# Moving the ranks' matmul to the state's PSUM bank, the row comparisons to GpSimd, and one transposition ahead of four

## The chip, the cores and the metric

The kernel runs on one core of one Trainium2 chip. The metric is the device time of one execution in microseconds. Four compute engines take part: TensorE (PE in the profile; PEld is its weight load), VectorE (DVE), ScalarE (ACT) and GpSimd (POOL). SyncE (SP) issues most of the DMAs.

## The reference

Three layers follow each other. The second routes each of 2304 token rows to one of eight experts; the third mixes all eight experts for each row.

```python
# q, k, v: (4, 8, 576, 64); x has 2304 rows of 512 columns; 8 experts, hidden width 1024
gamma = 1.0 - 2.0 ** (-5.0 - np.arange(H))
Dmat = np.where(rel >= 0, gamma[:, None, None] ** rel[None], 0.0)
x = (scale * (q @ k.T) * Dmat) @ v                   # retention, per batch and head
...
logits = x @ w_gate; e = argmax(logits)               # first mixture: the best expert
out[row] = softmax(logits)[e] * (relu(x[row] @ w1[e]) @ w2[e])
...
P = exp(logits2 - max); 8 rounds: P /= P.sum(1) + 1e-9; P /= P.sum(0) + 1e-9; P *= N / E
out += P[:, e:e+1] * (relu(x @ w1[e]) @ w2[e])        # second mixture: all experts
```

## The kernel before

The rows are worked in 18 tiles of 128 rows. The first sixteen (t = 0 to 15) are four chunks of each of the four batches, and carry a running state `st[b]` per batch; the last two hold the remaining 64 rows of two batches each. One loop over t runs the retention of tile t and, one tile behind it, the routing of tile t - 1. The order of the instructions on each engine is the order in which the program writes them: nothing is rearranged, and an engine that waits holds up all that stands behind it in its own queue.

One turn of the loop issues, in this order:

- `scale(t + 2)`: GpSimd multiplies k by its decays (L376) and q by its own (L379, `qs`), each over 128x512.
- `scores(t + 1)`: TensorE multiplies k and q (L391), VectorE applies the decay mask (L397, `sc`).
- `logits(t - 1)`: TensorE multiplies the tile's output by the gate's weights (L470) into columns 0 to 127 of PSUM bank 7; ScalarE copies them to `L` (L473).
- `states(t)`: TensorE applies the state to `qs` (L409), from the fifth tile on.
- `xtrans(t - 1)`: TensorE transposes the tile's output in four steps (L446) into bank 1.
- `route_a(t - 1)`: TensorE transposes `L` (L478) into columns 128 to 255 of bank 7. VectorE reduces it (L480), takes the maximum and its index (L483, L484, L486), makes the one-hot row `ohb` (L488) and the difference `sh` (L490).
- `new_state(t)`: TensorE multiplies k and v (L421) into bank 5; VectorE adds them to the state (L427, or a copy, L429, in the first chunk).
- `enlist(t - 2)`: TensorE collects the token numbers of an earlier tile from `at` and `row` (L532).
- `route_e(t - 1)`, `attend(t)`: ScalarE's exponential (L496), VectorE's gate (L497, L499); TensorE multiplies scores and v (L437), and ScalarE copies the result out (L440).
- `route_b(t - 1)`: two matmuls (L504, L505) count the rows per expert ahead of each row, into columns 256 to 271 of bank 7. VectorE turns the counts into a place (L510 to L513), splits it into `high` and `low` (L515 to L517) and makes two `row` tables of 24 columns (L523). GpSimd makes `at` over 128 columns (L521).
- `xout(t - 1)`: ScalarE scales the tile's output (L452), SP writes it to DRAM (L455).

From the twelfth tile on the same turns also split the first expert's weights into a high and a low part: ScalarE casts (L256), VectorE and GpSimd subtract half each (L233). After the loop, the first mixture's matmuls begin while the last tile's routing ends; then a table of the experts' order is made, and the rest of the weights are loaded.

A PSUM bank has one buffer. A new tile in a bank may be written only when all accesses to the tile before it are over. The lines touched here:

```python
p = d["pr"][:, 256:256 + 2 * E].rearrange("p (a e) -> p a e", a=2)   # route_b: bank 7, with the logits
nc.tensor.matmul(p[:, 0, :], ltb, d["ohb"], start=True, stop=True)
```

Of the kernel before, what the change touches and what calls it, by code (L numbers as in the profile page):

```python
# [13 lines left out]
ALU = mybir.AluOpType  # L14
# [21 lines left out]
def kernel(  # L36
# [18 lines left out]
    nc = tc.nc  # L55
    N, DM = out.shape
    E, _, F = w11.shape
    NT = N // 128
# [34 lines left out]
    def bank(i, shape=(128, 512)):  # L93
        return psum.tile(list(shape), F32, tag=f"b{i}", name=f"b{i}")
# [27 lines left out]
    tokf = const.tile([128, 2, NT], F32, name="tokf")  # L122
    places = const.tile([128, NT], F32, name="places")
    iota = const.tile([128, 128], F32, name="iota")
    tile0 = const.tile([128, E, 3], F32, name="tile0")
# [38 lines left out]
    def part(src, make):  # L164
        raws.append([src, make, None, 0])
        return len(raws) - 1
# [32 lines left out]
    for p in range(1):  # L199
        for e in range(E):  # L200
            for j in range(2):
                pr = [part((e, j, h), lambda e, j, h: w21[e][:, h * half + 256 * j:h * half + 256 * (j + 1)]
                           .rearrange("(k p) f -> p k f", p=128)) for h in range(2)]
# [104 lines left out]
    with ExitStack() as at:  # L308
# [7 lines left out]
        T = {}  # L316
# [53 lines left out]
        def scale(t):  # L370

            d = T[t]
            ch = t // B
            if ch < NCH:
                f = cs[:, C_KS + ch * H:C_KS + (ch + 1) * H].unsqueeze(2).to_broadcast([128, H, D])
                nc.gpsimd.tensor_tensor(d["k"], d["k"], f, ALU.mult)  # L376
            if ch:
                d["qs"] = wk.tile([128, 4, 128], F32, tag="qs", name="qs")
                nc.gpsimd.tensor_tensor(d["qs"], d["qT"], qdec[ch], ALU.mult)  # L379
# [20 lines left out]
        def states(t):  # L400

            d = T[t]
            ch = t // B
            d["xT"] = xp = bank(4 if t % 2 else 0, (128, 4, 128))
            if ch:
                for r in range(4):
                    off = 0
                    for b, s, n in tiles[t]:
                        nc.tensor.matmul(xp[:, r, off:off + n], st[b][:, r, :], d["qs"][:, r, off:off + n],  # L409
                                         start=r == 0 and off == 0, stop=False, skip_group_check=True)  # L410
                        off += n

        def new_state(t):

            d = T[t]
            ch = t // B
            if ch < NCH:
                sp = bank(5, (128, 4, 64))
                for h in range(H):
                    g = slice(64 * (h % 2), 64 * (h % 2) + 64)  # L420
                    nc.tensor.matmul(sp[g, h // 2, :], d["k"][:, h, :], d["v"][:, h, :], start=True, stop=True,  # L421
                                     tile_position=(0, 64 * (h % 2)))
                s = st[tiles[t][0][0]]
                for lo in (0, 64):
                    o = s[lo:lo + 64, :, lo:lo + 64]
                    if ch:
                        nc.vector.tensor_tensor(o, sp[lo:lo + 64], o, ALU.add)  # L427
                    else:
                        nc.vector.tensor_copy(o, sp[lo:lo + 64])  # L429
# [12 lines left out]
        def xtrans(t):  # L442
            d = T[t]
            d["xp"] = p = bank(1 if t < NT - 1 else 4, (128, 4, 128))
            for r in range(4):
                nc.tensor.transpose(p[:, r, :], d["xT"][:, r, :], ident)  # L446
# [18 lines left out]
        def logits(t):  # L465
            d = T[t]
            d["pr"] = bank(7)
            p = d["pr"][:, 0:128]
            for r in range(KB):
                nc.tensor.matmul(p[32 * r:32 * r + 32, :], wg1[:, r, :], d["xT"][:, r, :], start=True, stop=True,  # L470
                                 tile_position=(0, 32 * r))
            d["L"] = wk.tile([128, 128], F32, tag="L", name="L")
            nc.scalar.copy(d["L"], p)  # L473

        def route_a(t):
            d = T[t]
            p = d["pr"][:, 128:256]
            nc.tensor.transpose(p, d["L"], ident)  # L478
            lg = wk.tile([128, E], F32, tag="lgs", name="lgs")
            nc.vector.tensor_reduce(lg, p.rearrange("p (k e) -> p e k", k=4)[:, 0:E, :], AX.X, ALU.add)  # L480
            m8 = wk.tile([128, 8], F32, tag="m8", name="m8")
            i8 = wk.tile([128, 8], U32, tag="i8", name="i8")
            nc.vector.max(m8, lg)  # L483
            nc.vector.max_index(i8, m8, lg)  # L484
            fi = wk.tile([128, 1], F32, tag="fi", name="fi")
            nc.vector.tensor_copy(fi, i8[:, 0:1])  # L486
            ohb = d["ohb"] = wk.tile([128, E], BF16, tag="ohb", name="ohb")
            nc.vector.tensor_scalar(ohb, cs[:, C_EXP:C_EXP + E], fi, None, ALU.is_equal)  # L488
            sh = d["sh"] = wk.tile([128, E], F32, tag="sh", name="sh")
            nc.vector.tensor_scalar(sh, lg, m8[:, 0:1], None, ALU.subtract)  # L490
# [9 lines left out]

        def route_b(t):
            d = T[t]
            p = d["pr"][:, 256:256 + 2 * E].rearrange("p (a e) -> p a e", a=2)
            nc.tensor.matmul(p[:, 0, :], ltb, d["ohb"], start=True, stop=True)  # L504
            nc.tensor.matmul(p[:, 1, :], onesb, d["ohb"], start=True, stop=True)  # L505
            t1 = wk.tile([128, E], F32, tag="t1", name="t1")
            pf = places[:, t:t + 1]
            low = wk.tile([128, 1], F32, tag="low", name="low")
            high = wk.tile([128, 1], F32, tag="high", name="high")
            nc.vector.tensor_tensor(t1, p[:, 0, :], base, ALU.add)  # L510
            nc.vector.tensor_tensor(t1, t1, d["ohb"], ALU.mult)
            nc.vector.tensor_reduce(pf, t1, AX.X, ALU.add)
            nc.vector.tensor_tensor(base, p[:, 1, :], base, ALU.add)  # L513

            nc.vector.tensor_scalar(high, pf, -63.5, 1.5 * 2.0 ** 30, ALU.add, ALU.add)  # L515
            nc.vector.tensor_scalar(high, high, -1.5 * 2.0 ** 30, None, ALU.add)
            nc.vector.tensor_tensor(low, pf, high, ALU.subtract)  # L517

            d["at"] = wk.tile([128, 128], BF16, tag="at", name="at")
            d["row"] = wk.tile([128, 2, E, 3], BF16, tag="row", name="row")  # L520
            nc.gpsimd.tensor_scalar(d["at"], iota, low, None, ALU.is_equal)  # L521
            for i in range(2):
                nc.vector.tensor_scalar(d["row"][:, i], tile0, high, tokf[:, i, t:t + 1], ALU.is_equal, ALU.mult)  # L523

        listed = []

# [402 lines left out]
        for t in range(NT):  # L929
            if t + 2 < NT:  # L930
                scale(t + 2)
            if t == NT - 1:
                states(t)
            if t:
                scores(t + 1)
                logits(t - 1)
            if t < NT - 1:
                states(t)
            if t:
                xtrans(t - 1)  # L940
                route_a(t - 1)
            table_step()
            presplit(t, 0)
            new_state(t)
            table_step()
            presplit(t, 1)
            if t == NT - 1:
                gtrans(0, 0)
            if t > 1:
                enlist(t - 2)  # L950
                if t == GAT1:
                    first_ids(1)
            if t:
                route_e(t - 1)
            attend(t)
            if t + 2 < NT and len(tiles[t + 2]) > 1:

                nc.gpsimd.memset(sc[t % 2][0:64, :, :, 64:128], 0.0)
            if t:
                route_b(t - 1)  # L960
                if t == GAT1:
                    gather(0, 1, 2)
                if t < NT - 1:
                    xout(t - 1)
            if n_known[0]:
                n_known[0] = min(8, n_known[0] + KN[max(0, t - PICK_AT - 1)])
                load_more()
            if t == PICK_AT:
                table.append(early_table())
            if t == IDX0:  # L970
                first_ids(0)
            if t == GAT1 - 1:
                early_tokens()
            table_step()
            presplit(t, 2)
            load(t + 4)
            table_step()
            presplit(t, 3)
            if t == GAT0:
                gather(0, 0, 1)  # L980
# [332 lines left out]
    for g in range(n_unit):  # L1313
        pe, i = divmod(g, 4)
        p, e = divmod(pe, E)
# [163 lines left out]
    for s in range(E, n_exp):  # L1479
        p, e = divmod(s, E)  # L1480
# [254 lines left out]
    while ready:  # L1735
        t = ready.pop()
# [66 lines left out]
    while n_done < len(tasks):  # L1803
        moved = True
        while moved:
            moved = False
            while ends and ends[0][0] <= t_now + 1e-9:
                _, _, t = heapq.heappop(ends)
# [12 lines left out]
            for k in at:  # L1821
                if at[k] > t_now + 1e-9:
                    continue
                if k == "PE":
                    if n_pe[0] < len(line) and not waits[line[n_pe[0]]]:
                        t = line[n_pe[0]]
# [105 lines left out]
```

## Time and profile before

| what | value |
| --- | --- |
| time, median of 3 runs | 1841.89 us (1840.78 to 1845.59) |
| time of the profiled execution | 1840.57 us |
| its span, first to last instruction | 1838.7 us |
| PE busy, share of the span | 1803.2 us, 98% |
| DVE busy | 1235.5 us, 67% |
| ACT busy | 892.0 us, 49% |
| POOL busy | 567.3 us, 31% |
| mean granted TensorE clock | 0.998 |

The busy shares are averages over stages with different limits: the loop over the 18 tiles is the first 119 us or so, and what follows is the two mixtures. Times in the rows below are microseconds from the start of the span. The 1.87 us between the span and the execution's time lie around it.

### The profile page before, as it was taken

Reading aid. Unit: us, or ns where it says so; the run is one execution under the profiler, and the core shown is the slowest. Engines: PE = TensorE matmul, PEld = TensorE weight load, DVE = VectorE, ACT = ScalarE, POOL = GpSimd, SP = SyncE. Lnnn points to the kernel's source line nnn. Section 1 sums busy time; section 2 is a strip of 40 time slices with the busy share of each in tenths; the row PEclk is TensorE's granted clock in tenths of the full one; section 3 lists DMA queues with packets and bytes.
Section 4 is the critical chain, followed back from the end, with each engine's and each line's share of the span. In section 5 each row is a group of like instructions: output and inputs, shape, how many; then the busy total and the mean of one; then the engine's idle time right before and its main releaser. Section 6 shows DMA issues by size and latency. Waiting matters only on the chain.

```text
span 1838.7 us, 32928 instructions
## 1 busy us (share of the span) xinstructions
PE 1803.2 (98%) x12265; PEld 1721.5 (94%) x12265; DVE 1235.5 (67%) x2313; ACT 892.0 (49%) x1718; POOL 567.3 (31%) x582
## 2 busy tenths in 40 slices
PE   8889999999999999999999999999999999999998
PEld 7769999999899999999899999999999999999997
DVE  7984456547645554554467777778877777777778
ACT  2344456544434343434455555555655555555554
POOL 4455577532432323334311112111323111111212
PEclk9999999999999999999999999999999999999999
DMA  8755556564454556444755555655455545555540
GB/s 293 252 174 193 184 185 205 193 204 177 152 215 161 205 173 224 177 178 163 258 158 163 164 158 174 192 155 155 144 173 190 159 155 161 169 155 165 155 127 35
DMA packets 190455, 325.05 MB, mean 177 GB/s; under 512 B 20534, under 2 KB 93383, under 8 KB 190284
## 3 DMA queue, kind: packets, MB, share of 16 engines
q1 hardware_dynamic: 186716, 312.20, 52.0%
q0 software_dynamic: 3136, 9.95, 1.6%
q8 instruction: 99, 1.62, 0.4%
q10 hardware_dynamic: 432, 0.69, 0.1%
q14 instruction: 72, 0.59, 0.1%
HBM read 248.26 MB, written 74.53 MB: 176 GB/s over the span
## 4 chain that ended last, share of the span: by engine, by line
PE 85%; DVE 3%; issue 2%; ACT 1%; POOL 0%; DMA 0%; POOLq 0%; ACTq 0%; DVEq 0%
PE b L1507 8%; PE b L1508 8%; PE b L1509 8%; PE b L1655 8%; PE b L1656 8%; PE b L1654 8%; PE b L1154 5%; PE b L1155 5%; PE b L1156 5%; PE b L1224 4%; PE b L1226 4%; PE b L1225 4%; PE b L705 3%; PE b L706 3%; PE b L707 3%
## 5 line engine op out<-in xcount | busy, mean ns | idle before, releaser
L1655 PE MATMUL b<-wb,sq 128*128 128x256 f32 x1344 | 379.1, 282 | 1.1 <-DVE wb L233 1.1
L1654 PE MATMUL b<-wb,sq 128*128 128x256 f32 x1344 | 378.6, 282 | 0.9 <-DVE a L1676 0.9
L1656 PE MATMUL b<-wb,sq 128*128 128x256 f32 x1344 | 378.9, 282 | 0.4 <-DVE sq L233 0.4
L1655 PEld LDWEIGHTS b<-wb,sq 128*128 128x128 f32 x1344 | 254.7, 190 | 1.7 <-DVE wb L233 1.7
L1654 PEld LDWEIGHTS b<-wb,sq 128*128 128x128 f32 x1344 | 254.5, 189 | 1.8 <-issue 1.3
L1656 PEld LDWEIGHTS b<-wb,sq 128*128 128x128 f32 x1344 | 254.6, 189 | 0.6 <-DVE sq L233 0.6
L233 POOL TENSOR_TENSOR ring<-raw,ring 128x256 fp32r<-128x256 f32 x192 | 172.1, 908 | 262.7 <-ACT ring L256 210.4
L233 DVE TENSOR_TENSOR sq<-hq,sq 128x768 fp32r<-128x768 f32 x167 | 169.9, 1021 | 69.1 <-ACT sq L1600 68.9
L233 DVE TENSOR_TENSOR ring<-raw,ring 128x256 fp32r<-128x256 f32 (+1 forms) x256 | 153.1, 601 | 83.5 <-ACT ring L256 73.8
L1412 POOL TENSOR_TENSOR raw<-raw,raw 128x512 f32<-128x512 f32 x60 | 83.3, 1389 | 387.5 <-DVE wb L233 316.3
L1522 ACT ACTIVATE hq<-hq 128x384 f32<-128x384 f32 x144 | 75.6, 525 | 187.5 <-DVE hq L1519 187.1
L1507 PE MATMUL b<-ch,wa 128*128 128x384 f32 x448 | 152.0, 339 | 2.4 <-DVE hq L1519 0.9
L1224 PE MATMUL b<-ch,ring 128*128 128x384 f32 x448 | 153.2, 342 | 0.1
L1507 PE MATMUL b<-c,wa 128*128 128x384 f32 x448 | 151.6, 338 | 1.0 <-ACT u L1513 1.0
L1600 ACT CAST sq<-hq 128x768 fp32r<-128x768 f32 x167 | 137.7, 830 | 29.7 <-PE b L1655 25.7
L1509 PE MATMUL b<-c,wa 128*128 128x384 f32 x448 | 151.1, 337 | 0.0
L1509 PE MATMUL b<-ch,wa 128*128 128x384 f32 x448 | 151.1, 337 | 0.0
L1508 PE MATMUL b<-cl,wa 128*128 128x384 f32 x448 | 151.0, 337 | 0.0
L1508 PE MATMUL b<-c,wa 128*128 128x384 f32 x448 | 151.0, 337 | 0.0
L1226 PE MATMUL b<-ch,ring 128*128 128x384 f32 x448 | 151.0, 337 | 0.0
L1154 PE MATMUL b<-ring,HH 128*128 128x512 f32 x384 | 150.7, 393 | 0.0
L1225 PE MATMUL b<-cl,ring 128*128 128x384 f32 x448 | 150.6, 336 | 0.0
(257 smaller groups left out, 4359.1 us busy)
## 6 DMA issues: line engine op xcount, KB each, us to landing
wa<-w1s SPq DMA_DIRECT2D x192, 512.0 KB
raw<-in_moe_w_dram SPq DMA_DIRECT2D x128, 512.0 KB
w1s<-ring SPq DMA_DIRECT2D x64, 896.0 KB
raw<-in_moe_w_dram SPq DMA_DIRECT2D x106, 256.0 KB
wa<-w1s SPq DMA_DIRECT2D x64, 256.0 KB
sums<-in_moe_w_dram SPq DMA_DIRECT2D x22, 256.0 KB
kT<-in_kT_dram SPq DMA_DIRECT2D x18, 256.0 KB
qT<-in_qT_dram SPq DMA_DIRECT2D x18, 256.0 KB
```

The source lines that it names most:

```text
L233: eng.tensor_tensor(lo, x, hi.bitcast(F32), ALU.subtract)
L1154: nc.tensor.matmul(y[t], hh[:, s], w.hi[:, f0:f0 + 512], start=first, stop=False)
L1224: nc.tensor.matmul(ps, a, xh[:, r, :], start=first and r == 0, stop=False, skip_group_check=True)
L1225: nc.tensor.matmul(ps, a, xl[:, r, :], start=False, stop=False, skip_group_check=True)
L1226: nc.tensor.matmul(ps, b, xh[:, r, :], start=False, stop=r == 1, skip_group_check=True)
L1507: nc.tensor.matmul(ps, a, xh[:, r, :], start=first, stop=False, skip_group_check=True)
L1508: nc.tensor.matmul(ps, a, xl_[:, r, :], start=False, stop=False, skip_group_check=True)
L1509: nc.tensor.matmul(ps, b, xh[:, r, :], start=False, stop=r == 1, skip_group_check=True)
L1600: nc.scalar.copy(o.tile[0], src.tile)
L1654: nc.tensor.matmul(ps, hh[:, r, c], wh[:, r], start=st, stop=False, skip_group_check=True)
L1655: nc.tensor.matmul(ps, hh[:, r, c], wl[:, r], start=False, stop=False, skip_group_check=True)
L1656: nc.tensor.matmul(ps, hl[:, r, c], wh[:, r], start=False, stop=kh == 1 and r == 1, skip_group_check=True)
```

## The change

Three edits. The ranks' two matmuls in `route_b(t - 1)` write columns 256 to 271 of bank 5, in the tile that `new_state(t)` has taken for the state's products (columns 0 to 255), in place of bank 7, where the logits are; the last tile takes bank 5 anew. The two `row` comparisons go from VectorE's queue to GpSimd's, behind `at`. The transposition of the logits, with all of `route_a`, is issued ahead of the four transpositions of the tile's output.

```diff
@@ new_state
+            pb = d["pb"] = bank(5)
             if ch < NCH:
-                sp = bank(5, (128, 4, 64))
+                sp = pb[:, 0:256].rearrange("p (r c) -> p r c", r=4)
@@ route_b
-            p = d["pr"][:, 256:256 + 2 * E].rearrange("p (a e) -> p a e", a=2)
+            p = T[t + 1]["pb"] if t + 1 < NT else bank(5)
+            p = p[:, 256:256 + 2 * E].rearrange("p (a e) -> p a e", a=2)
...
             nc.gpsimd.tensor_scalar(d["at"], iota, low, None, ALU.is_equal)
             for i in range(2):
-                nc.vector.tensor_scalar(d["row"][:, i], tile0, high, tokf[:, i, t:t + 1], ALU.is_equal, ALU.mult)
+                nc.gpsimd.tensor_scalar(d["row"][:, i], tile0, high, tokf[:, i, t:t + 1], ALU.is_equal, ALU.mult)
@@ the loop over t
             if t:
+                route_a(t - 1)
                 xtrans(t - 1)
-                route_a(t - 1)
```

## Rows read from the trace of the kernel before

**Rows 1.** Busy time by stage: length, PE, PEld, DVE, ACT, POOL, clock, DMA, GB/s.
```profile
0.00:119.30 119.30, 101.91 (x1329) 85.46 (x1330) 99.66 (x435) 37.94 (x101) 55.93 (x68) 0.99 0.78 254
...
160.00:1838.70 1678.70, 1665.90 (x10739) 1604.83 (x10739) 1110.40 (x1814) 832.77 (x1577) 490.68 (x490) 1.00 0.52 171
```

**Rows 2.** Timeline of one ordinary turn: start, duration, engine, line, operation, [idle before <- releaser].
```profile
59.18 0.16 DVE L517 TENSOR_TENSOR low<-places,high 128x1 f32<-128x1 f32 x1
59.25 0.58 DVE L523 TENSOR_SCALAR row<-tile,high,tokf 128x24 bf16<-128x24 f32 x2
...
59.27 1.16 PE L409 MATMUL b<-qs,st 128*128 128x128 f32 x8
...
59.44 0.60 POOL L521 TENSOR_SCALAR at<-iota,low 128x128 bf16<-128x128 f32 x1 [2.64 <-PE b L470]
...
59.75 1.27 DVE L397 TENSOR_TENSOR sc<-b,cm 128x512 f32<-128x512 f32 x2
...
60.01 1.05 POOL L376 TENSOR_TENSOR k<-k,cs 128x512 f32<-128x512 f32 x1
...
60.70 0.27 PE L478 MATMUL b<-cs,L 128*128 128x128 f32 x1
...
61.01 1.28 POOL L379 TENSOR_TENSOR qs<-qT,qdec 128x512 f32<-128x512 f32 x1
61.01 0.19 DVE L480 TENSOR_REDUCE lgs<-b 128x8 f32<-128x32 f32 x1
...
61.91 0.41 DVE L488 TENSOR_SCALAR ohb<-cs,fi 128x8 bf16<-128x8 f32 x1
62.23 0.22 DVE L490 TENSOR_SCALAR sh<-lgs,m 128x8 f32<-128x8 f32 x1
62.36 0.85 DVE L427 TENSOR_TENSOR st<-b,st 64x256 f32<-64x256 f32 x2
...
62.69 0.18 PE L504 MATMUL b<-ohb,ltb 128*128 128x8 bf16 x1
...
62.83 1.16 PE L391 MATMUL b<-qT,kT 64*128 64x128 f32 x16
...
64.40 0.43 PE L470 MATMUL b<-xT,wg 128*32 128x128 f32 x8 [0.41 <-DVE high L515]
...
64.67 0.16 DVE L517 TENSOR_TENSOR low<-places,high 128x1 f32<-128x1 f32 x1
```

**Rows 3.** The same view, DVE: the row that marks a turn, at five tiles.
```profile
19.52 0.16 DVE L517 TENSOR_TENSOR low<-places,high 128x1 f32<-128x1 f32 x1
...
70.16 0.16 DVE L517 TENSOR_TENSOR low<-places,high 128x1 f32<-128x1 f32 x1
...
76.63 0.16 DVE L517 TENSOR_TENSOR low<-places,high 128x1 f32<-128x1 f32 x1
...
83.78 0.16 DVE L517 TENSOR_TENSOR low<-places,high 128x1 f32<-128x1 f32 x1
...
115.32 0.16 DVE L517 TENSOR_TENSOR low<-places,high 128x1 f32<-128x1 f32 x1
```

**Rows 4.** Timeline of the longest turn, GpSimd and VectorE.
```profile
79.26 1.04 POOL L376 TENSOR_TENSOR k<-k,cs 128x512 f32<-128x512 f32 x1 [1.77 <-DMA k<-in_k_dram]
79.36 0.97 DVE L488 TENSOR_SCALAR ohb<-cs,fi 128x8 bf16<-128x8 f32 x1
80.25 1.31 DVE L490 TENSOR_SCALAR sh<-lgs,m 128x8 f32<-128x8 f32 x1
80.27 1.27 POOL L379 TENSOR_TENSOR qs<-qT,qdec 128x512 f32<-128x512 f32 x1
```

**Rows 5.** GpSimd's scalar operations by line: count, busy us, mean ns, idle before.
```profile
L521 POOL TENSOR_SCALAR at<-iota,low 128x128 bf16<-128x128 f32 x18 | 11.0, 609 | 44.5 <-DVE low L517 25.2 <-PE b L470 19.2
...
L1182 POOL TENSOR_SCALAR a<-a,P 128x512 f32<-128x512 f32 x3 | 4.7, 1564 | 2.0 <-DVE P L1134 2.0
```

**Rows 6.** Timeline of the last turn, TensorE.
```profile
116.31 0.21 PE L532 MATMUL b<-row,at 128*128 128x24 bf16 x2 [0.24 <-POOL at L521]
```

## The prediction

> **What bounds the kernel now.** I read the busy time by stage first. From 160 us to the end TensorE is busy 1665.90 of 1678.70 us, while in the first 119.30 us it is busy 101.91 and VectorE 99.66 [rows 1]. The three edits all lie in that first stage, so what they are worth is what they do to the 18 turns of its loop; everything behind it starts from the loop's last results and moves with them. The timeline of an ordinary turn shows what sets its length [rows 2]. I measure a turn from one `low` (L517) to the next: 59.18 to 64.67, 5.49 us. Read VectorE's rows: `low`, the two `row` (0.58), the mask (1.27), the reduction of the logits at 61.01, `ohb` at 61.91, `sh`, the state's addition from 62.36, and so on without a gap until the next `low`. TensorE has a gap: L470 stood still for 0.41 us until the places' arithmetic, the readers of bank 7, was done. So VectorE's queue is the bound, with TensorE just behind it: L478 ends at 60.97, and the reduction that reads it starts at 61.01, as the mask ends at 61.02.
>
> One more thing is to be seen in these rows. `ohb` takes 0.41 us, `sh`, of the same form, 0.22. `ohb` ends at 62.32, and GpSimd's `qs` at 62.29. In the longest turn this is plain [rows 4]: `ohb` starts in GpSimd's k product and ends at 80.33, 0.03 after that ends (80.30); `sh` starts at 80.25 and ends at 81.56, 0.02 after `qs` (81.54). These small VectorE operations from SBUF to SBUF stand still until the GpSimd instruction under way is over; one gets through between k and `qs`, the next does not. The mask, whose one input is in PSUM, runs 1.27 us beside the same GpSimd work unharmed [rows 2]. So in an ordinary turn a second chain already touches the bound: `low`, `at`, k, `qs`, `ohb`.
>
> **The change part by part.**
>
> *The ranks' bank.* It removes L470's wait, 0.41 us of TensorE in a turn. It adds one: L504 writes the tile from whose other columns L427 reads. The program orders all accesses to one PSUM tile, so I take it that L504 stands behind L427, which ends at 62.36 + 0.85 = 63.21, in place of 62.69. Behind L504 in TensorE's queue stand L391, L470, L409 and, after the third edit, L478. The loop that this makes: 0.85 for the state, 0.05 to L504 (an estimate, from the 0.04 that lie between the end of L478, 60.97, and the reduction that reads it), 0.14 to L391 (62.69 to 62.83), 1.16, 0.43, 1.16 for L409, 0.27 for L478: 4.06 from the state to the reduction. From there to the state's next addition it is 62.36 - 61.01 = 1.35, less the 0.19 by which `ohb` exceeds `sh`: 1.16. Together 5.22 us. That is under 5.49, so the new wait does not bound a turn; it limits what can be gained to 0.27. If the framework let the two run at once, TensorE would be freer still, by 0.52 (62.69 to 63.21), and nothing else changes.
>
> The Trainium skill's page "PSUM — Partial Sum Buffer", section "PSUM bank collisions raise a hardware error", says that two engines may not touch one bank and 32-partition quadrant at the same time, other columns or not. By it the wait of L504 for L427 is a must and the sum is the one with 5.22; no row here shows two engines in one bank.
>
> *The logits' transposition.* It saves the reduction the four transpositions ahead of it: L409 starts at 59.27 and takes 1.16, so L478 could start near 60.43 in place of 60.70. Its cover is `L`, which ScalarE has copied long before in every turn with L409. The four transpositions of x come 0.27 later; their reader is `xout`, a turn away, and I cost that at nothing.
>
> *The row comparisons.* VectorE loses 0.58 us less the 0.08 by which neighbours overlap: the mask starts 0.50 earlier, near 59.25, ends near 60.52, and the reduction follows L478, near 1.4 after `low`, in place of 1.83. GpSimd gains two instructions between `at` and k. The trace before has no such row, so I bound it. GpSimd's scalar operation takes 609 ns over 128 columns and 1564 over 512 [rows 5]: 2.49 ns a column and 0.29 us fixed, hence 0.35 us for 24 columns. Lower bound: 24 x 2.49 ns = 0.06 us, were the fixed part hidden; upper bound: the 0.609 of `at`, since a second operand and operation come in. I take 0.35 for each, 0.70 for both, the estimate that rests on the same kind of instruction.
>
> The Trainium skill's "GPSIMD Engine Reference", section "Engine selection", calls one-input work on GpSimd roughly line-rate, which at its 1.2 GHz is 0.83 ns a column. By that rule 0.50 of `at` would be fixed, a `row` would take an estimated 0.52 and the whole sum come near +9 us; the two widths above do not agree with it, at 2.49 ns.
>
> Now what is late next. k starts at 60.01, 0.83 after `low`; with two rows ahead of it 1.53 after, and `qs` ends at 62.29 + 0.70, 3.81 after `low`. VectorE comes to `ohb` near 2.3 after `low`, in the middle of k (1.53 to 2.57); it gets through as k ends, and `sh` stands until `qs` is over, as in the longest turn. There the state's addition starts 0.07 before `qs` ends: here it would start at 3.74 after `low`, in place of 62.36 - 59.18 = 3.18. From the state to the next `low` is 64.67 - 62.36 = 2.31. A turn becomes 6.05 us in place of 5.49. In other words, the 0.50 that VectorE saves and the 0.41 of TensorE go into a longer wait for GpSimd, and 0.56 on top.
>
> **The sum over the turns** [rows 3]. Nine turns, 19.52 to 70.16, take 50.64 us; among them two in which GpSimd waits for k's DMA and which are already near 6.0. Nine of 6.05 are 54.45: +3.8. The turn 70.16 to 76.63 (6.47) makes the early table on VectorE; it starts 0.50 earlier and then meets `qs`: about -0.3. The turn 76.63 to 83.78 (7.15) is late because k lands 2.63 after `low` and stops both `ohb` and `sh`. In the new kernel `ohb` comes near 2.3, about when k lands: between 5.3 (both get ahead of k) and 6.9 (both stopped), I take 6.25, -0.9. The five turns 83.78 to 115.32 (31.54) have GpSimd's share of the weight split behind the rows, but for two of them no k; 0.70 more on GpSimd against 0.50 less on VectorE, some of it hidden behind the casts: +0.8, between -1 and +2. In the last turn L532 already waits 0.24 for `at` [rows 6], and then for two `row` as well, with the last logits' transposition behind it on TensorE: +0.7. Sum: 3.8 - 0.3 - 0.9 + 0.8 + 0.7 = +4.1 us. The profiled execution took 1840.57, so 1844.7; the median of the runs is 1.3 above that execution, so 1846.
>
> **The rivals.**
>
> *Faster: GpSimd's chain does not bind.* If the two `row` add under 0.14 us to GpSimd's chain (`qs` may end that much later and the state still starts at 3.18), or if `ohb` and `sh` slip through, the turn falls to the loop of 5.22. For it: 0.91 us of waiting is taken from two engines. Against it: both rows with a stopped operation, and 0.29 us fixed for a GpSimd scalar operation. Its time: nine turns 47.0, -3.7; the table's turn -0.6; the longest -1.9; five of -0.27, -1.3; the end +0.7: -6.8, 1835.
>
> *Slower still: a `row` costs what `at` does.* Then 1.14 us stand ahead of k (0.57 each, with overlap), a turn is 6.49: +7.8 for nine, +0.2, -0.6, +1.5, +1.1: +10, 1852. For it: two operands and two operations; against it: 24 columns.
>
> *No difference: the loop is not what the rest waits for.* If the mixture's start hides some of it behind loads, or the intervals with DMA waits absorb the rows, the sum is 0 to 2, 1842 to 1844. Against it: the expert table needs the last tile's places.
>
> **How the numbers follow.** The forecast 0.56, rows as dear as `at` 0.20, faster 0.14, no difference 0.10. The likeliest gives 1846, with 1842.5 to 1850 as its own range. The range 1835 to 1854 reaches to both rivals' ends, since the cost of a `row` and what GpSimd stops are unknown costs of both signs. About 0.3%, 5.5 us, is what a measurement of this kernel can tell from no change: slower takes the 0.20 and somewhat under a third of the forecast, 0.36; faster 0.13; within it the rest, 0.51.
>
> **What would show it.** L470 without a wait for VectorE, and L504 with one for L427. L523 on POOL with 0.35 us each. k 0.7 later after `low`; `ohb` and `sh` together over 1.2 us in an ordinary turn, ending with `qs`; turns near 6.05. I am wrong if a `row` takes 0.1 us, or if `ohb` runs 0.23 beside `qs`: then turns are near 5.2, and the time falls.

## The result, and the profile after

The changed kernel took 1852.13 us (median of 4 runs, 1851.33 to 1854.92) against 1841.93 for the kernel before beside it: a ratio of 1.0054, with a 95% interval of 1.0038 to 1.0070. It became slower, by about 10 us where +4 was forecast; the time lies inside the forecast's range of 1835 to 1854, near its upper end, and above the 1842.5 to 1850 that the likeliest case had for itself.

The edits move the line numbers: from the state's on each is one higher than before, from inside `route_b` on two higher: L470 is now L471, L478 L479, L488 `ohb` L489, L490 `sh` L491, L427 L428, L504 L506, L517 `low` L519, L521 `at` L523, L523 `row` L525, L532 L534.

The timeline of an ordinary turn of the kernel after, VectorE, GpSimd and two matmuls (start, duration, engine, line, operation, [idle before <- releaser]), answers to [rows 2]:

```profile
62.05 0.43 PE L471 MATMUL b<-xT,wg 128*32 128x128 f32 x8
...
62.61 0.16 DVE L519 TENSOR_TENSOR low<-places,high 128x1 f32<-128x1 f32 x1
62.69 1.28 DVE L397 TENSOR_TENSOR sc<-b,cm 128x512 f32<-128x512 f32 x2
62.95 0.60 POOL L523 TENSOR_SCALAR at<-iota,low 128x128 bf16<-128x128 f32 x1 [2.96 <-DVE low L519]
63.53 0.87 POOL L525 TENSOR_SCALAR row<-tile,high,tokf 128x24 bf16<-128x24 f32 x2
63.88 0.18 DVE L481 TENSOR_REDUCE lgs<-b 128x8 f32<-128x32 f32 x1
...
64.36 1.04 POOL L376 TENSOR_TENSOR k<-k,cs 128x512 f32<-128x512 f32 x1
...
64.76 0.67 DVE L489 TENSOR_SCALAR ohb<-cs,fi 128x8 bf16<-128x8 f32 x1
65.34 1.31 DVE L491 TENSOR_SCALAR sh<-lgs,m 128x8 f32<-128x8 f32 x1
65.36 1.26 POOL L379 TENSOR_TENSOR qs<-qT,qdec 128x512 f32<-128x512 f32 x1
...
66.56 0.85 DVE L428 TENSOR_TENSOR st<-b,st 64x256 f32<-64x256 f32 x2
...
67.47 0.17 PE L506 MATMUL b<-ohb,ltb 128*128 128x8 bf16 x1 [1.58 <-DVE st L428]
...
68.87 0.16 DVE L519 TENSOR_TENSOR low<-places,high 128x1 f32<-128x1 f32 x1
```

Read it from `low` to `low`: 6.26 us, where [rows 2] had 5.49. VectorE comes to the reduction 1.27 after `low` in place of 1.83, so the 0.56 that it was to gain is there. It loses it in two instructions: `ohb` ends at 65.43, 0.03 after k (65.40), and `sh` at 66.65, 0.03 after `qs` (66.62). (`sh` is recorded from 65.34, 0.02 ahead of `qs`, but `ohb` is then still under way.) Together they stand 1.89 us between the start of `ohb` and the end of `sh`, for work that takes 0.23 and 0.22 when it is left alone. The matmul of the ranks, L506, starts 0.06 after the state's second addition ends (67.41). L471 waits for nothing on VectorE.

The groups of GpSimd's operations up to 132 us, by line (count, then busy us and mean ns, then idle before), answer to [rows 5]:

```profile
L525 POOL TENSOR_SCALAR row<-tile,high,tokf 128x24 bf16<-128x24 f32 x36 | 15.7, 447 | 0.0
L523 POOL TENSOR_SCALAR at<-iota,low 128x128 bf16<-128x128 f32 x18 | 11.2, 623 | 40.0 <-DVE low L519 26.8 <-DVE sums L570 5.6 <-DVE sums L593 2.8
```

A `row` on GpSimd is 447 ns, between the estimate of 0.35 and the upper bound of 0.609.

To see where the 10 us lie I took the start of every `low`, 18 of them, and split the execution at them as the forecast did: nine turns, the turn with the early table, the longest turn, the five turns with the weight split, the last, what follows the last `low` to the end of the span, and what lies ahead of the first. All values in us, differences of starts in the profiled executions:

| stretch | before | after | difference | forecast |
| --- | --- | --- | --- | --- |
| ahead of the first `low` | 19.52 | 19.27 | -0.25 | 0 |
| nine turns | 50.64 | 56.06 | +5.42 | +3.8 |
| table turn | 6.47 | 6.41 | -0.06 | -0.3 |
| longest turn | 7.15 | 5.59 | -1.56 | -0.9 |
| five turns | 31.54 | 37.04 | +5.50 | +0.8 |
| last turn | 3.89 | 4.70 | +0.81 | +0.7 |
| after the loop | 1719.49 | 1720.63 | +1.14 | 0 |
| span | 1838.7 | 1849.7 | +11.0 | +4.1 |

Half of the loss is the ordinary turns, as forecast and somewhat larger. The other half is the five turns. What happens there is in the windows of the kernel after (start:end length, then busy us of PE, PEld, DVE, ACT and POOL, granted clock, DMA share, GB/s): all five turns, an ordinary turn, and three stretches of the five turns:

```profile
87.33:124.37 37.04, 31.29 (x329) 26.66 (x328) 29.73 (x119) 13.19 (x35) 21.41 (x32) 0.82 0.60 197
62.60:68.90 6.30, 4.72 (x73) 4.10 (x72) 5.87 (x21) 1.72 (x5) 3.68 (x5) 1.00 0.76 254
93.10:99.70 6.60, 6.17 (x46) 5.22 (x47) 4.66 (x23) 1.98 (x4) 3.38 (x6) 0.50 0.66 200
103.00:110.10 7.10, 4.98 (x77) 4.27 (x73) 6.57 (x24) 2.67 (x8) 4.71 (x7) 1.00 0.56 185
110.20:116.80 6.60, 6.60 (x45) 6.18 (x39) 4.19 (x16) 1.25 (x5) 4.26 (x6) 0.50 0.74 230
```

From 103.00 TensorE is busy 4.98 of 7.10 us; from 110.20 its granted clock is 0.50, which is 1.2 GHz of its 2.4, and then it is busy every bit of 6.60 us. Over the five turns the mean granted clock is 0.82. The same five turns of the kernel before had 0.95, with one stretch at 0.50 from 84.9 to 88.2:

```profile
83.78:115.32 31.54, 27.20 (x335) 22.91 (x327) 28.37 (x129) 13.16 (x34) 16.46 (x21) 0.95 0.70 226
```

The kernel after has two more stretches at half clock, from about 69.0 to 72.3, in the ninth turn, and from about 171.5 to 174.5, where TensorE is busy throughout and the kernel before has none. Nor is it this execution alone: the mean granted clock is 0.992 to 0.996 in the four runs of the kernel after, and 0.996 or more in 43 of the 48 runs of the kernel before that were taken beside the experiments.

Where TensorE is slow, VectorE waits for it, and no longer only the other way round. The ranking of waits of the kernel after up to 132 us (engine, line, released by: total us, times, longest) holds TensorE's wait for the state, but also one in which VectorE waits for TensorE's transposition of the logits, and one at L534 for `row`:

```profile
PE b L506 <- DVE st L428: 9.9, 8, 2.1
DVE lgs L481 <- PE b L479: 7.4, 5, 2.0
...
PE b L534 <- POOL row L525: 1.5, 3, 1.1
```

### The profile page after: what moved, and what is told of

The parts are those of the page before. It is cut to its first block, busy times and chain, and to the rows that moved or that the text cites. A ratio compares the mean times of both kernels' runs of the same rounds, so it can differ in the third digit from the quotient of the medians.

```text
span 1849.7 us, 32940 instructions
## 1 busy us (share of the span) xinstructions
PE 1806.1 (98%) x12265; PEld 1725.3 (93%) x12265; DVE 1238.9 (67%) x2277; ACT 891.6 (48%) x1718; POOL 580.3 (31%) x618
## 4 chain that ended last, share of the span: by engine, by line
PE 85%; DVE 2%; issue 2%; DMA 1%; ACT 0%; POOL 0%; POOLq 0%; ACTq 0%; DVEq 0%
PE b L1509 8%; PE b L1510 8%; PE b L1511 8%; PE b L1657 8%; PE b L1656 8%; PE b L1658 8%; PE b L1156 5%; PE b L1157 5%; PE b L1158 5%; PE b L1226 4%; PE b L1228 4%; PE b L1227 4%; PE b L707 3%; PE b L709 3%; PE b L708 3%
```

## The experiments

### The row comparisons back on VectorE; the row comparisons alone

Two kernels cut the change in two. In the first the ranks stay in bank 5 and the logits' transposition stays early, but `row` is made on VectorE again; the second is the kernel before with nothing but the rows moved.

```diff
-                nc.gpsimd.tensor_scalar(d["row"][:, i], tile0, high, tokf[:, i, t:t + 1], ALU.is_equal, ALU.mult)
+                nc.vector.tensor_scalar(d["row"][:, i], tile0, high, tokf[:, i, t:t + 1], ALU.is_equal, ALU.mult)
```

> The changed kernel with the two row comparisons back on VectorE; the ranks' bank and the order of the transpositions stay changed. Theory A (GpSimd's chain at, row, row, k, qs stops the subtraction sh, and the longer waits let TensorE's clock fall): k starts again 0.83 us after low, an ordinary turn is 5.4 to 5.5 us, and the time is that of the kernel before, 1839 to 1843. Rival B (the matmul of the ranks, which now waits for the state's addition, sets the turn): the wait is still there, turns stay near 6.2, 1849 or more.

> The kernel before with only the row comparisons moved to GpSimd. Theory A: k starts 1.7 us after low, sh waits for qs, turns 6.1 to 6.3, 1848 to 1853, nearly the whole loss. Rival B: without the shared bank nothing is lost; VectorE has 0.5 us less to do, turns 5.2 to 5.5, 1836 to 1842.

Rows back: 1842.14 us against 1842.65, ratio 0.9998 (0.9989 to 1.0006). Rows alone: 1852.32, ratio 1.0054 (1.0039 to 1.0068). The whole loss comes from the two comparisons, and the other two edits together are worth nothing that shows. Nine turns take 51.24 and 57.49 us, against 50.64 before and 56.06 after.

With the rows alone it is another instruction that stands. An ordinary turn of that kernel (47.19 to 53.60) takes 6.41 us, more than the 6.1 to 6.3 expected:

```profile
49.91 1.33 DVE L488 TENSOR_SCALAR ohb<-cs,fi 128x8 bf16<-128x8 f32 x1
49.95 1.27 POOL L379 TENSOR_TENSOR qs<-qT,qdec 128x512 f32<-128x512 f32 x1
51.16 0.22 DVE L490 TENSOR_SCALAR sh<-lgs,m 128x8 f32<-128x8 f32 x1
```

The reduction comes 1.83 after `low` here, as its transposition is not early, so `ohb` comes as k ends (49.98); it stands through `qs`, and `sh`, behind it, takes its 0.22. The cause is the same, the victim is not the one that was expected.

The timeline of one turn of the first kernel (rows back), 42.45 to 47.67, in which both of GpSimd's products come late:

```profile
43.02 1.28 DVE L397 TENSOR_TENSOR sc<-b,cm 128x512 f32<-128x512 f32 x2
...
43.60 0.27 PE L479 MATMUL b<-cs,L 128*128 128x128 f32 x1
...
43.93 1.04 POOL L376 TENSOR_TENSOR k<-k,cs 128x512 f32<-128x512 f32 x1 [0.63 <-DMA k<-in_k_dram]
44.21 0.17 DVE L481 TENSOR_REDUCE lgs<-b 128x8 f32<-128x32 f32 x1
...
45.09 0.23 DVE L489 TENSOR_SCALAR ohb<-cs,fi 128x8 bf16<-128x8 f32 x1
45.23 0.23 DVE L491 TENSOR_SCALAR sh<-lgs,m 128x8 f32<-128x8 f32 x1
...
46.87 1.28 POOL L379 TENSOR_TENSOR qs<-qT,qdec 128x512 f32<-128x512 f32 x1 [1.89 <-DMA qdec<-in_decays_dram]
...
47.67 0.49 DVE L519 TENSOR_TENSOR low<-places,high 128x1 f32<-128x1 f32 x1
```

k ends at 44.97 and `qs` starts only at 46.87, as its decays land late; `ohb` and `sh` fall into the hole and take 0.23 each. The turn is 5.22 us, the length that the forecast gave for the loop through bank 5, but that is chance: the reduction starts at 44.21 as the mask ends, 0.34 after the transposition it reads is done (L479, 43.87), so this turn is as long as VectorE's own queue, and TensorE does not hold it up. The new bank wait allows less still: the kernel without `sh`, below, which has it too, has turns of 4.86 to 5.01. And the hole is not free: `low` then stands until the late `qs` is over (48.15), and the next turn takes 6.44.

### Without `sh`

On the changed kernel, the difference of logits and maximum over 8 columns is taken inside ScalarE's exponential, with the negated maximum as its bias; VectorE makes that over one column.

```diff
-            nc.vector.tensor_scalar(sh, lg, m8[:, 0:1], None, ALU.subtract)
+            nc.vector.tensor_scalar(nm, m8[:, 0:1], -1.0, None, ALU.mult)
...
-            nc.scalar.activation(ex, d["sh"], AF.Exp, accum_out=sm)
+            nc.scalar.activation(ex, d["lg"], AF.Exp, bias=d["nm"], accum_out=sm)
```

> The changed kernel without the subtraction sh over 8 columns: VectorE negates the maximum (one column) and ScalarE's exponential takes it as its bias. Same result, one column in place of eight. Theory A: the one-hot row still gets through as k ends, about 2.8 us after low, the negation is not stopped by qs (operations on one column run 0.15 us beside it), the state follows near 2.95: turns of 5.25 to 5.4, 1838 to 1844. Rival B: the ranks' matmul still waits for the state; if that set the turn, it would stay near 6.2, 1849 or more.

1839.45 us, ratio 0.9987 (0.9978 to 0.9996): the loss is gone, and a little more. Nine turns take 46.61, 5.18 a turn, a little under the 5.25 expected at least. The timeline of a turn of this kernel (5.10 us):

```profile
58.20 1.04 POOL L376 TENSOR_TENSOR k<-k,cs 128x512 f32<-128x512 f32 x1
...
58.60 0.67 DVE L489 TENSOR_SCALAR ohb<-cs,fi 128x8 bf16<-128x8 f32 x1
59.18 0.14 DVE L491 TENSOR_SCALAR nm<-m 128x1 f32<-128x1 f32 x1
59.20 1.27 POOL L379 TENSOR_TENSOR qs<-qT,qdec 128x512 f32<-128x512 f32 x1
59.25 0.85 DVE L428 TENSOR_TENSOR st<-b,st 64x256 f32<-64x256 f32 x2
```

`ohb` still stands until k is over (59.27 against 59.24), but behind it nothing waits for `qs`: the state's addition starts 2.80 after `low`, in place of 3.95, and runs its 0.85 in the midst of `qs`. GpSimd's queue is as long as in the changed kernel; only the instruction that it stopped is gone.

### `row` ahead of `at`

```diff
-            nc.gpsimd.tensor_scalar(d["at"], iota, low, None, ALU.is_equal)
             for i in range(2):
                 nc.gpsimd.tensor_scalar(d["row"][:, i], tile0, high, tokf[:, i, t:t + 1], ALU.is_equal, ALU.mult)
+            nc.gpsimd.tensor_scalar(d["at"], iota, low, None, ALU.is_equal)
```

> The changed kernel with the two row comparisons ahead of at on GpSimd; they need high, which is ready some 0.2 us before low. Theory A: k and qs come 0.15 to 0.2 us earlier, sh still waits for qs, and an ordinary turn falls from 6.26 to 6.05 to 6.15; over nine turns 1 to 2 us, 1849 to 1852. If GpSimd's start is not what counts, 6.26.

`at` is issued behind the two `row`, which need only `high`, one instruction earlier than `low`. 1850.53 us, ratio 1.0051 (1.0037 to 1.0065); the ordinary turn is 6.09 us, as expected. `row` starts 0.07 after `low` instead of 0.92, k 1.49 in place of 1.75: k 0.26 earlier, the turn 0.17 shorter. Before, here and after, `qs` ends 3.11, 3.77 and 4.01 us after `low`, and the ordinary turns are 5.49, 6.09 and 6.26. The nine turns take 53.51, 2.55 less than in the changed kernel, but the five turns 38.84, 1.80 more, at a mean granted clock of 0.74. In the time over all this is no difference from the changed kernel that can be told: the intervals of the two ratios overlap.

### Twice the rows

Two more comparisons, into a tile that nobody reads, follow the two `row` on GpSimd: some 0.9 us of added work in each turn, on the engine that the ordinary turn waits for.

```diff
+            r2 = wk.tile([128, 2, E, 3], BF16, tag="row2", name="row2")
+            for i in range(2):
+                nc.gpsimd.tensor_scalar(r2[:, i], tile0, high, tokf[:, i, t:t + 1], ALU.is_equal, ALU.mult)
```

> The changed kernel with each row comparison made twice on GpSimd, the second time into a tile that nothing reads: two more instructions of about 0.42 us in every turn. Theory A: k starts some 2.6 us after low in place of 1.75, and every ordinary turn grows by that dose, from 6.26 to 7.0 to 7.2, unless the one-hot row comes before k has begun (it comes 2.36 after low): then only sh or qs is met and the turn grows less. In all 8 to 14 us over the changed kernel, 1860 to 1866. If GpSimd's chain is not what sets a turn, no change.

The expected time was missed: 1850.06 us (1845.43 to 1859.59), ratio 1.0039 (1.0022 to 1.0056), no slower than the change itself. Nine turns take 50.69, as before the change. The timeline of an ordinary turn of this kernel (47.42 to 53.04, 5.62 us) shows why:

```profile
49.58 0.23 DVE L489 TENSOR_SCALAR ohb<-cs,fi 128x8 bf16<-128x8 f32 x1
49.72 0.22 DVE L491 TENSOR_SCALAR sh<-lgs,m 128x8 f32<-128x8 f32 x1
...
50.06 1.04 POOL L376 TENSOR_TENSOR k<-k,cs 128x512 f32<-128x512 f32 x1
51.06 1.27 POOL L379 TENSOR_TENSOR qs<-qT,qdec 128x512 f32<-128x512 f32 x1
...
51.32 1.04 DVE L513 TENSOR_TENSOR t<-t,ohb 128x8 f32<-128x8 f32 x1
```

k starts 2.64 after `low`, so `ohb` and `sh` are past before it. Now `qs` stops another instruction, the product of the counts with `ohb` (L513), whose two inputs lie in SBUF: 1.04 us for a work of 0.17. In the table turn and the longest, where `ohb` came nearer to k, `sh` stood again, 1.30 us in the one, through `qs`, and 2.38 in the other, through k and `qs`; each took 7.1, the five turns 39.40 and the last 5.82, so that little of the gain is left in the time. More work on GpSimd gave shorter ordinary turns: what counts is which of VectorE's instructions meet k and `qs`, not how busy GpSimd is.

### Filler matmuls, to keep TensorE's clock up

Sixteen matmuls whose result nobody reads, ahead of each ranks' matmul (L506): in all turns, and in a second kernel only for tiles 8 to 13.

```diff
+            for _ in range(16 if 8 <= t <= 13 else 0):
+                nc.tensor.matmul(d["pr"][:, 272:400], onesb, onesb, start=True, stop=True)
             nc.tensor.matmul(p[:, 0, :], ltb, d["ohb"], start=True, stop=True)
```

> The changed kernel with 16 matmuls of 128 columns that nothing reads, in each turn, ahead of the ranks' matmul, where TensorE waits for the state's addition. Theory C (part of the loss is TensorE's clock, which falls to half after turns in which it waits): no stretch of the loop shows a granted clock under 1, the reductions' waits for the logits' transposition (7.4 us in all, 5 times) shrink to under 3, and the time falls by 3 to 5 us to 1847 to 1849; ordinary turns stay 6.26. If the clock costs nothing, 1852 as before.

> The changed kernel with the 16 unread matmuls ahead of the ranks' matmul in the routing of tiles 8 to 13 alone, so that the last turns and what follows stay as they were. Theory C (the clock): no stretch at half clock between the ninth turn and the end of the loop, the five split turns take 33 to 34 us in place of 37.0, the last turn 4.7; the time falls by 2 to 4 us to 1848 to 1850, if the wait behind the loop does not draw a stretch at half clock of its own. If that stretch comes again near 140 us, 1851 to 1854.

In both, the five turns run at full clock and take 33.34 and 33.08 us in place of 37.04. In both, the time did not fall, where 1847 to 1849 was expected of the first: 1853.36, ratio 1.0057 (1.0042 to 1.0071), and 1853.36, ratio 1.0065 (1.0051 to 1.0078). Windows of the second, ahead of the loop's first `low` (21.72) and over the five turns:

```profile
15.30:21.90 6.60, 6.21 (x61) 4.94 (x61) 5.29 (x20) 1.74 (x5) 1.90 (x2) 0.50 0.79 296
...
91.29:124.37 33.08, 28.16 (x371) 23.58 (x363) 30.11 (x119) 13.55 (x36) 20.99 (x31) 1.00 0.67 216
```

The half-clock stretch was gone from the five turns, but others stood elsewhere: behind the loop, near 145 us, in both kernels, and in the second also ahead of the loop (first `low` at 21.72, not 19.27). The fillers can't have made that one, as they come much later; it differs from execution to execution, and the kernel with the rows back has one from about 10.7 to 14.1 us. In the first kernel the stretch after the loop is 3.8 us longer than in the changed kernel; in the second 2.4 to 3.5 us of each execution lie outside the span, against 1.7 to 1.8 in the changed kernel. So the clock makes the five turns long, by 3.7 to 4.0 us in these profiled executions. That it makes the whole execution longer is not shown: the first kernel has a mean granted clock of 0.997 in all five runs, against 0.992 to 0.996 in the changed kernel, and is no faster. What the kernel would be without any half-clock stretch and without fillers, no run shows.

### VectorE's small operations taken off SBUF

If the stopped instructions are the cause, it should be possible to have the rows on GpSimd at no loss. On the changed kernel, the reduction now writes the logits into PSUM (bank 7, columns 256 to 263, which the ranks had left); the one-hot row comes from comparing them with the maximum, which also drops the index search and its cast; the subtraction goes into the exponential, as above. Three kernels: with the rows on VectorE, on GpSimd, and on VectorE with the ranks back in bank 7.

```diff
-            lg = wk.tile([128, E], F32, tag="lgs", name="lgs")
+            lg = d["pr"][:, 256:256 + E]
...
-            nc.vector.tensor_scalar(ohb, cs[:, C_EXP:C_EXP + E], fi, None, ALU.is_equal)
+            nc.vector.tensor_scalar(ohb, lg, m8[:, 0:1], None, ALU.is_equal)
```

> The changed kernel with the rows back on VectorE and without any VectorE operation of 8 columns from SBUF to SBUF between the logits and the state: the reduced logits stay in PSUM (bank 7, columns 256 to 263), the one-hot row compares them with their maximum (the index search and its cast go), and the exponential takes the negated maximum as bias. Theory A: neither the one-hot row nor what follows meets qs any more; VectorE's chain is 4.9 us, TensorE's own work 5.03, turns 5.0 to 5.15, no stretch of the loop at half clock, 1831 to 1836. If the stop is not bound to operands in SBUF, the one-hot row ends with k or qs again and turns are 5.4 or more.

> The same with the rows on GpSimd, as in the changed kernel. Theory A: k and qs end as late as in the changed kernel (qs 4.0 us after low), but hold up nothing but the product of two SBUF tiles in the places' arithmetic; turns 5.0 to 5.2, 1831 to 1838. If GpSimd's rows cost a turn in any other way (their results late for TensorE), turns stay above 5.5.

> The version with the logits in PSUM and the rows on VectorE, but with the ranks back in bank 7, behind the logits, so that the next logits wait for the places' arithmetic again. If the ranks' bank is worth what VectorE's stops had hidden, this is slower by 0.2 to 0.4 us a turn, 3 to 6 us; if TensorE is busy at that point anyhow (its own work 5.03 us a turn), within 1 us of the version with bank 5.

All three beat the kernel before and the changed one: 1834.48, ratio 0.9959 (0.9943 to 0.9975); 1834.23, 0.9952 (0.9940 to 0.9965); 1833.89, 0.9957 (0.9944 to 0.9970). They can't be told from each other: here neither the place of the rows nor the bank of the ranks is worth anything. Nine turns take 45.33, 45.30 and 45.87. The gain has two sources that these kernels don't part: no instruction is stopped ahead of the state, and VectorE's chain is shorter without the search. From the start of the maximum to that of `ohb` it is 0.21 us (56.52 to 56.73 in the turn below), where with the search it is 0.67 (44.42 to 45.09 in the turn with the rows back). The timeline of a turn with the rows on GpSimd:

```profile
55.80 0.88 POOL L522 TENSOR_SCALAR row<-tile,high,tokf 128x24 bf16<-128x24 f32 x2
...
56.63 1.05 POOL L376 TENSOR_TENSOR k<-k,cs 128x512 f32<-128x512 f32 x1
...
56.73 0.23 DVE L485 TENSOR_SCALAR ohb<-b,m 128x8 bf16<-128x8 f32 x1
56.87 0.14 DVE L487 TENSOR_SCALAR nm<-m 128x1 f32<-128x1 f32 x1
...
57.34 0.86 DVE L428 TENSOR_TENSOR st<-b,st 64x256 f32<-64x256 f32 x2 [0.33 <-PE b L422]
```

`ohb` takes 0.23 us in the middle of k; and the state's addition waits 0.33 for TensorE's products and no longer for what stands in VectorE's own queue. The bound has gone to TensorE, as the window of this kernel from 24 to 65 us shows, in which it is busy 39.98 of 41.00 us:

```profile
24.00:65.00 41.00, 39.98 (x589) 33.09 (x585) 34.98 (x138) 14.64 (x41) 29.76 (x40) 1.00 0.90 302
```

## Why the prediction was right, and where it was off

**The mechanism held.** The row comparisons left VectorE, GpSimd's `qs` came later, and `sh` stood until it was over (`ohb` in its place where the transposition is not early). Rows alone and rows back put the whole loss on this edit, and the kernel without `sh` takes it away with GpSimd's queue unchanged. The forecast said that turns are bound by `low`, `at`, the rows, k, `qs`, and from there 2.31 us to the next `low`; the turn measured has exactly 2.31 (66.56 to 68.87).

The Trainium skill's page "SBUF — State Buffer", section "Who interferes with whom", has the rule for this: VectorE shares a pair of SBUF ports with GpSimd, an operation of a scalar form from SBUF to SBUF or one with two SBUF inputs may need it, and whoever comes first holds it for the whole instruction while the other waits. The traces agree: `ohb` and `sh` end 0.03 after k and `qs`, L513 with two SBUF inputs stood 1.04, and with the logits in PSUM `ohb` took 0.23 beside k.

**A row's cost** was 0.447, not 0.35. In the turn shown, `at` starts 0.34 after `low` (0.26 before), and the two rows take 0.83 to k's start, so k comes 1.75 after `low` and not 1.53; the state's addition 3.95 and not 3.74; the turn is 6.26 and not 6.05. Nine times 0.21 are 1.9, somewhat more than the step from +3.8 to +5.4, as the first of the nine took only 5.46. The estimate came from two widths of an operation with one scalar per partition; a `row` has two operations and two such scalars, and cost 0.1 more than the widths give. Which of the two makes the 0.1 was not tried.

**The step that failed in size is "+0.8, between -1 and +2" for the five turns: they cost +5.5.** The term was made of GpSimd's and VectorE's work alone. That part came out within its bounds: with fillers, at full clock, the five turns take 33.08 to 33.34, which is 1.5 to 1.8 above before, and 1.9 to 2.1 above the 31.22 of the kernel with the rows back, which has no stretch at half clock there. The other 3.7 to 4.0 is TensorE's clock, for which the forecast had no term, although the kernel before also shows a stretch at half clock in those turns. When VectorE stands for GpSimd, TensorE stands for VectorE; after a stretch in which it was busy 4.98 of 7.10 us its granted clock fell to 0.50, and at 1.2 GHz its own work, 6.60 of 6.60 us, became the bound. That the waits let the clock fall is the order in which these rows stand; the fillers, which took waiting time away, kept the clock up in these turns, but such stretches stood elsewhere, and the time was no lower. That the time still lies inside the range owes something to luck: the range reached up to 1854 for dearer rows, not for this.

**The bank edit and the early transposition** did as forecast: L471's wait went, L506 waits for the state (0.06 after its end), and the reduction comes early, at the mask's end. The loop through bank 5 was taken too long, though: 5.22, where the kernel without `sh` has turns of 4.86 to 5.01. The forecast added whole durations on TensorE, but neighbours overlap: in the turn with the rows back L391 (46.39, 1.16 long) is followed by L471 at 47.48, L409 at 47.84 and L479 at 48.83, and from the state's start (45.36) to the end of L479 (49.10) it is 3.74, where the forecast had 4.06. This loop bound no turn, so the sum did not suffer. With the rows back the two edits are worth 0.9998. They were not run one by one.

**The small terms.** The longest turn gained 1.56 and not 0.9, as `ohb` and `sh` (84.10 and 84.24, 0.23 each) both got ahead of k (85.59), which the forecast had as the short end, 5.3, and met by a middle value; the table turn gained 0.06 and not 0.3. The last turn lost 0.81, forecast 0.7: L534 waited for `row`, and the kernels with rows on VectorE have 3.88 to 3.91 there, those with rows on GpSimd 4.57 to 5.82. The 1.1 us behind the loop stay open; the half-clock stretch at 171.5 to 174.5, where TensorE is busy throughout, may be part of it. That stretch behind the loop varies between 1718.0 and 1724.4 in these kernels' profiles.

**The rivals.** "Slower still" gave 1852, the time measured, but that is chance: it needed a turn of 6.49 and had +1.5 for the five turns. "Faster" needed `ohb` and `sh` to slip past. The kernel without `sh` shows some of what that is worth (1839.45 against 1842.65); the 8.7 us of the kernel with the logits in PSUM and the rows on GpSimd (1842.97 less 1834.23) are more than that, as its chain is also shorter by the search.

## What to carry to other kernels

Before a small operation is moved from VectorE to GpSimd, look at which of VectorE's instructions will then run beside GpSimd's long ones: an operation over 8 columns from SBUF to SBUF can cost 1.3 us in place of 0.22, so freeing an engine of 0.5 us may cost it more. Folding one such instruction into another engine's work took the whole loss away here (ratio 0.9987 in place of 1.0054); giving the other its input from PSUM too, and dropping the index search, made the kernel 0.4 to 0.5% faster than before, and the place of the moved work indifferent. When a loop becomes longer through waits, give the forecast a term for TensorE's clock in the stretches where TensorE is nearest to the bound: here the five turns lost 3.7 to 4.0 us to it.

## What the runs showed that was not expected

- More GpSimd work can shorten a turn: four `row` gave 5.62 us a turn and two 6.26, since k then starts behind `ohb` and `sh`.
- An operation of the same form over one column (`nm`) goes through: 0.14 us beside `qs` and, in the last timeline, in the midst of k, where one over eight columns (`sh`) stood 1.31 beside `qs`. One column is not enough by itself: `low`, with two inputs in SBUF, stood 0.49 until `qs` was over, in place of 0.16.
- In one turn of the changed kernel (62.23) VectorE stood 0.41 us ahead of `high` behind L515, its own instruction, while nothing else in the trace points to a releaser; it comes at the same tile in several of these kernels, and stays open.
